# Second network's second product in an attention and two-network kernel: seven products for eight on the last two superblocks, in a phase of its own

## The chip, the cores and the metric

One NeuronCore of one Trainium2 chip runs the whole kernel in one launch. The metric is device time in microseconds (us) of that core. Lower is better. The kernel before was timed in three runs: 848.94, 844.0 and 844.74 us, a median of 844.74.

## The reference, cut to what matters

The reference computes a linear attention over 2304 tokens (4 batches of 576), and puts the result through two feed-forward networks, one after the other. The change is in the last line of the second network.

```python
def _moe2_ref(x, w_in, w_out):            # x: 2304 x 512
    h = x @ w_in                          # 512 x 2048
    sp = np.where(h > 20.0, h, np.log1p(np.exp(np.minimum(h, 20.0))))
    g = h * np.tanh(sp)                   # "mish"
    return (g @ w_out).astype(np.float32) # 2048 x 512
```

The weights arrive as 64-bit floats; the kernel decodes them on the chip.

## The kernel before

**Precision.** TensorE multiplies in a rounded 32-bit type (`float32r`). Every operand is therefore split in two tiles, a rounded value (hi) and what the rounding left (lo), by `split` (L408): a copy that rounds (ACT or DVE), then a subtraction (DVE, seldom POOL). A product is three matmuls: hi·hi, hi·lo, lo·hi (`SPLIT`, L258). Decoded weights lie in the tiles `W` (L267): 16 tiles, one for each 128 of the 2048 hidden columns, each with a half for the first weight (`io` 0; in the second network ring and scratch) and a half for the second weight (`io` 1), hi and lo.

**Stages.** Attention runs first and in pieces beside the first network. The first network's first three token blocks (512 tokens each) run plainly (L933, L976). From then on the work is 32 steps, `n` = 0 to 31 (the loop at L1404). A step is one superblock of 768 tokens by 256 hidden columns (`NPR` = 8 steps to a superblock). Steps 0 to 7 are the last 768 tokens of the first network; steps 8 to 31 are the second network, superblocks 0, 1 and 2. The steps that the change treats differently are 16 to 31.

**A step.** The first matrix product of a step is cut in blocks of two by two, and takes seven block products where the plain rule has eight (`product`, L1154). Each has 6 matmuls of 384 columns. `after` (L1203) takes the sums out of PSUM on DVE (L1213) and ACT (L796); `activated` (L1179) applies the activation on ACT (L1185) and splits the result into the tiles `second` and `g`. Between the products of step n stand the matmuls of the second product for step n-1: `gemm_out2` (L1236), six groups `c` of 128 tokens, each 6 matmuls of 512 columns, which add up in six PSUM banks over the eight steps of a superblock:

```python
        def mm():
            for j in range(2):
                for i, (a, b) in enumerate(SPLIT):
                    nc.tensor.matmul(
                        out=bank_of(out_banks[c]),
                        lhsT=g_tile(n, j)[:, a, c * P : (c + 1) * P],
                        rhs=w_mm(2 * pr + j, 1, b, 0, 512),
```

After the eighth step, `out_evac` (L1299) copies a bank to SBUF and stores it.

**What a step loads.** The seven sums of blocks of the first weight are made earlier, kept in DRAM (`combos`) and streamed back in each superblock: three loads of 512 KB and one of 256 KB for a step (`ring_load`, L1132), into a ring of tiles that holds two steps. A load waits for the products of the step that used the tile before. The step's other operands, sums of token blocks, are made once a superblock (`x_load` L1042, `x_sums` L1063, `x_split` L1076).

**What sets the order.** The program does not issue as it is written. Every operation is recorded with the keys it reads and writes and a cost (`Plan`, L20). A list scheduler then orders all of them over the engines, six times over with different urgencies, and the order with the earliest planned end is issued (`best`, L169). On TensorE a common key, `spine`, keeps the steps' matmuls in the order of the text; the other engines' order is the scheduler's. All DMAs go through SP's one queue, in order (`dma`, L328). A DMA, or an engine's instruction, that waits holds up what is queued behind it.

Of the kernel before, what the change touches and what calls it, by code (L numbers as in the profile page):

```python
# [210 lines left out]
def tile_attention_moe_moe(  # L211
# [55 lines left out]
    W = [const.tile([P, 2, 1024], F32R, name=f"W{i}") for i in range(NFC - NLATE)]  # L267
# [8 lines left out]
    combos = dram.tile([NFC, P, 3584], F32, name="combos")  # L276

# [38 lines left out]
    def f32(t):  # L316
        return t.bitcast(F32)

# [93 lines left out]
    def weight(m, io, fc):  # L412
# [3 lines left out]
        late = [("late",)] if fc >= NFC - NLATE else []  # L416
        split(
            512,
            lambda: W[fc][:, io, 0:512],
            lambda: W[fc][:, io, 512:1024],  # L420
# [14 lines left out]
    def keep(j, n):  # L435
# [4 lines left out]
        w0, w1 = [lambda k=k: f32(W[2 * j + k][:, 0, :]) for k in range(2)]  # L440
# [12 lines left out]
    def combine1(j, n):  # L453
# [5 lines left out]
        w0, w1 = [lambda k=k: f32(W[2 * j + k][:, 0, :]) for k in range(2)]  # L459
# [85 lines left out]
    def w_mm(fc, io, part, c, n=P):  # L545
        return W[fc][:, io, part * 512 + c * P : part * 512 + c * P + n]
# [450 lines left out]
    second = []  # L997

    def pool_first():
        sctx.close()  # L1000
        late = ctx.enter_context(tc.tile_pool(name="late", bufs=1, side="right", reuse_waits="tile"))
        W.extend(late.tile([P, 2, 1024], F32R, name=f"W{i}") for i in range(NFC - NLATE, NFC))
# [36 lines left out]
    def xf(i):  # L1039
        return f32(W[i][:, 0, 0 : 2 * NB])  # L1040

    def x_load(sb):  # L1042
        for i, (c, half) in enumerate(((0, 0), (1, 0), (0, 1), (1, 1))):
# [8 lines left out]
                w_keys(i),  # L1052
                lambda i=i: xf(i).rearrange("p (c n) -> p c n", c=2),
# [9 lines left out]
    def x_sums():  # L1063
        differ(2 * NB, ta, lambda: xf(1), lambda: xf(0), w_keys(0) + w_keys(1), tak)
        differ(2 * NB, tb, lambda: xf(3), ta, w_keys(3) + tak, tbk)

    def operand(k, a):
        if k in (2, 3):
            fc = ((4, 5), (6, 7))[k - 2][a]
            return W[fc][:, 0, 0 : 2 * NB].rearrange("p (c n) -> p c n", c=2)  # L1070
# [5 lines left out]
    def x_split(k, fresh):  # L1076
        old, new = [], [("second",)]
        if fresh and k in (2, 3):
# [9 lines left out]
        if k == 3:  # L1088
            for c in range(2):
# [3 lines left out]
                    NB, t, lambda cut=cut: xf(3)[:, cut], lambda cut=cut: xf(1)[:, cut], w_keys(1) + w_keys(3) + new, tk  # L1093
# [12 lines left out]
            0: (lambda: xf(0), w_keys(0)),  # L1106
            1: (tb, tbk),
            2: (lambda: xf(2), w_keys(2)),
            4: (ta, tak),
            5: (tb, tbk),  # L1110
            6: (lambda: xf(3), w_keys(3)),
# [10 lines left out]
        if k == 1:  # L1122
            differ(2 * NB, tb, tb, lambda: xf(2), w_keys(2), tbk)

    def ring(n, u):
        if u < 3:
            fc = 8 + 3 * (n % 2) + u
            return fc, 0, 512, w_keys(fc)
        fc = NFC - 2 + n % 4 // 2
        return fc, n % 2 * 512, 256, [("W", 0, fc, n % 2)]  # L1130

    def ring_load(n, u):  # L1132
        if n >= NP:
            return
        fc, at_, half, keys = ring(n, u)
        dma(
            P * half * 8,
            [("combo", n if n < NPR else NPR + n % NPR, u)],
            keys,
            lambda: f32(W[fc][:, 0, at_ : at_ + 2 * half]),  # L1140
            lambda: combos[n if n < NPR else NPR + n % NPR][:, u * 1024 : u * 1024 + 2 * half],
        )
# [11 lines left out]
    def product(n, k):  # L1154
        u, q = PLACE[k]
        fc, at_, half, wk = ring(n, u)
        key = bank(n, k)

        def mm():
            for cc in range(2):  # L1160
                for i, (a, b) in enumerate(SPLIT):
                    w = at_ + a * half + q * 256 + cc * P
                    nc.tensor.matmul(  # L1163
                        out=bank_of(key)[:, 0:NB],
                        lhsT=W[fc][:, 0, w : w + P],
# [13 lines left out]
    def activated(n, j, half, t, tk):  # L1179
# [8 lines left out]
        act(NB + 1540 * first, tk + ([] if first else tables), tk + (tables if first else []), fn)  # L1188
        gk = [[("gg", n % 2, j, half, a)] for a in range(2)]
# [13 lines left out]
    def after(n, k):  # L1203
# [5 lines left out]
        def added(name, of, op=ALU.add):  # L1209
# [255 lines left out]
```

## Time and profile before

| | |
|---|---|
| median of three runs (lowest, highest) | 844.74 us (844.0, 848.94) |
| the profiled execution's own time | 846.24 us |
| its span, first to last instruction | 844.5 us |
| TensorE busy, granted clock | 830.8 us, 0.997 |
| VectorE (DVE), ScalarE (ACT), GpSimd (POOL) busy | 570.6, 430.6, 14.8 us |
| moved by DMA | 153.89 MB |

The engines run side by side, and each works through its own queue in order. The span is set by the chain of work that ends last; an engine's busy time matters only where that chain runs through it. Matmuls overlap in the records, so what one matmul costs is read from the distance between the starts of two, not from its recorded length.

### The profile page before, as it was taken

To read this page: it belongs to the slowest core of one execution; us is meant where nothing else is said; L and a number is where in the kernel's file an instruction comes from. 1 tells how busy PE (TensorE), PEld (TensorE's weight loads), DVE (VectorE), ACT (ScalarE), POOL (GpSimd) and SP (SyncE) were. 2 spreads that over 40 slices of the span, in tenths; PEclk is the share of its full clock that TensorE was granted. 3 is DMA by queue.
4 is the path that set the end of the run, shared out by engine and by line. 5 is a ranking of instruction groups with operands and counts; after the bars stand their busy time and mean duration, and the time that the engine had idled before them with its cause. 6 is when DMAs were issued, how large, how long until landed. Compare 5 with 4: busy or idle time off the path is not lost.

```text
span 844.5 us, 12240 instructions
## 1 busy us (share of the span) xinstructions
PE 830.8 (98%) x4463; PEld 715.7 (85%) x4463; DVE 570.6 (68%) x1038; ACT 430.6 (51%) x851; POOL 14.8 (2%) x21
## 2 busy tenths in 40 slices
PE   8999999999999999999999999999999999999997
PEld 7787677887778888999999998898898998988985
DVE  6999995979969777566779889456333365334331
ACT  5988894345555445444556755344423345323222
POOL 0001010010000000000000000000000000000000
PEclk9999999999999999999999999999999999999998
DMA  9687762635476577865888887445534335434202
GB/s 272 172 249 258 215 220 95 202 110 161 128 212 222 192 260 250 252 223 174 288 282 273 282 267 224 131 140 183 177 113 118 120 113 156 156 112 137 76 1 75
DMA packets 99451, 153.89 MB, mean 182 GB/s; under 512 B 35136, under 2 KB 68672, under 8 KB 99392
## 3 DMA queue, kind: packets, MB, share of 16 engines
q1 hardware_dynamic: 99392, 153.12, 58.4%
q8 instruction: 35, 0.57, 0.3%
q14 instruction: 24, 0.20, 0.1%
HBM read 112.72 MB, written 40.37 MB: 181 GB/s over the span
## 4 chain that ended last, share of the span: by engine, by line
PE 81%; DVE 13%; DMA 2%; issue 2%; ACT 1%; SPq 0%; ACTq 0%; DVEq 0%
PE at L1163 27%; PE acc L1243 16%; PE acc L976 10%; PE h L933 9%; PE h L1243 8%; PE acc L1268 5%; PE h L1268 3%; DVE dec L400 2%; DVE dec L405 2%; DVE dec L393 1%; DVE W L339 1%; DVE gt L952 1%; DVE pmt L594 1%; PE at L852 1%; PE acc L612 1%
## 5 line engine op out<-in xcount | busy, mean ns | idle before, releaser
L1163 PE MATMUL at<-xt,W 128*128 128x384 f32 x954 | 191.3, 335 | 0.0
L1163 PEld LDWEIGHTS at<-xt,W 128*128 128x128 f32 x954 | 169.6, 188 | 12.6
L933 PE MATMUL h<-xt,W 128*128 128x512 f32 x576 | 149.4, 401 | 2.7 <-DVE W L339 1.0
L976 PE MATMUL acc<-g,W 128*128 128x512 f32 x576 | 146.4, 397 | 0.4 <-DVE W L339 0.4
L933 PEld LDWEIGHTS h<-xt,W 128*128 128x128 f32 x576 | 105.6, 188 | 28.6 <-DVE W L339 1.9
L1185 ACT ACTIVATE stage<-stage 128x384 f32<-128x384 f32 x94 | 49.2, 524 | 156.8 <-DVE stage L1213 156.7
L976 PEld LDWEIGHTS acc<-g,W 128*128 128x128 f32 x576 | 106.5, 188 | 23.6 <-DVE W L339 0.8
L1243 PE MATMUL acc<-W,second 128*128 128x512 f32 x432 | 115.6, 394 | 0.0
L1243 PEld LDWEIGHTS acc<-W,second 128*128 128x128 f32 x432 | 79.7, 188 | 10.6
L1213 DVE TENSOR_TENSOR stage<-at,stage 128x384 f32<-128x384 f32 x91 | 50.0, 554 | 50.9 <-PE at L1163 50.6
L1163 PE MATMUL at<-W,W 128*128 128x384 f32 x372 | 74.7, 335 | 0.0
L339 DVE TENSOR_TENSOR second<-stage,second 128x384 fp32r<-128x384 f32 x70 | 38.9, 556 | 44.3 <-ACT second L347 44.1
L1163 PEld LDWEIGHTS at<-W,W 128*128 128x128 f32 x372 | 65.9, 188 | 2.9
L1243 PE MATMUL h<-W,second 128*128 128x512 f32 x216 | 57.6, 394 | 0.0
L347 ACT ACTIVATE g<-gt 128x512 fp32r<-128x512 f32 (+1 forms) x56 | 34.4, 614 | 38.4 <-PE acc L976 33.3
L339 DVE TENSOR_TENSOR g<-gt,g 128x512 fp32r<-128x512 f32 (+1 forms) x52 | 34.6, 665 | 21.0 <-ACT g L347 20.5
L1185 ACT ACTIVATE gt<-gt 128x384 f32<-128x384 f32 x34 | 17.8, 524 | 58.1 <-DVE gt L1213 58.0
L356 ACT ACTIVATE dec<-raw 128x512 f32<-128x512 f32 x63 | 42.0, 667 | 7.3 <-DMA raw<-in_moe_w_in_dram 3.9
L947 ACT ACTIVATE gt<-h 128x512 f32<-128x512 f32 x48 | 28.5, 594 | 32.3 <-PE h L933 30.3
L405 DVE CUSTOM_DVE_ANT_0 dec<-raw,dec 128x1024 uint16<-128x1024 uint16 x64 | 43.7, 683 | 1.5
L1243 PEld LDWEIGHTS h<-W,second 128*128 128x128 f32 x216 | 39.9, 188 | 5.4
L400 DVE SCALAR_TENSOR_TENSOR dec<-raw,dec 128x512 int32<-128x512 int32 x64 | 43.8, 685 | 0.7
(141 smaller groups left out, 1098.5 us busy)
## 6 DMA issues: line engine op xcount, KB each, us to landing
W<-combos SPq DMA_DIRECT2D x96, 512.0 KB, 3.7
raw<-in_moe_w_in_dram SPq DMA_DIRECT2D x32, 512.0 KB, 5.0
raw<-in_moe_w_out_dram SPq DMA_DIRECT2D x32, 512.0 KB, 4.7
combos<-raw SPq DMA_DIRECT2D x32, 512.0 KB, 3.3
W<-combos SPq DMA_DIRECT2D x32, 256.0 KB, 3.7
combos<-raw SPq DMA_DIRECT2D x24, 256.0 KB, 3.5
kt<-in_k_dram SPq DMA_DIRECT2D x16, 288.0 KB, 4.3
W<-x2d SPq DMA_DIRECT2D x12, 384.0 KB, 3.9
```

The costliest lines, as they stand in the source:

```text
L339: return lambda: engine.tensor_tensor(out=out(), in0=in0(), in1=in1(), op=op)
L347: (ACT, act_ns(n), lambda: nc.scalar.activation(out=out(), in_=in_(), func=AF.Copy), False),
L356: (ACT, act_ns(512), lambda: nc.scalar.activation(out=out, in_=in_, func=AF.Copy, scale=scale), False),
L400: lambda: nc.vector.scalar_tensor_tensor(out=a, in0=hi_w, scalar=-0x80000000, in1=a, op0=ALU.bitwise_and, op1=ALU.bitwise_or),
L405: dve(512, [rl], [da], lambda: nc.vector.tensor_tensor(out=a, in0=a, in1=lo_w, op=ALU.add), pair=True)
L933: nc.tensor.matmul(out=h(), lhsT=w_mm(fc, 0, a, cc), rhs=x_of(t)[:, cc, b, :], start=cc == 0 and i == 0, stop=cc == NCC - 1 and i == 2,)
L976: nc.tensor.matmul(out=acc[dm][:, 0:nb], lhsT=w_mm(fc, 1, a, dm), rhs=g_of(n)[:, b, :], start=fc == 0 and i == 0, stop=fc == NFC - 1 and i ...
L1163: nc.tensor.matmul(out=bank_of(key)[:, 0:NB], lhsT=W[fc][:, 0, w : w + P], rhs=operand(k, b)[:, cc, :], start=cc == 0 and i == 0, stop=cc ...
L1185: nc.scalar.activation(out=t(), in_=t(), func=AF.Mish if n >= NPR else AF.Gelu_apprx_sigmoid)
L1213: dve(NB, [key, sk], tk, lambda: nc.vector.tensor_tensor(out=t(), in0=in0(), in1=in1(), op=op))
L1243: nc.tensor.matmul(out=bank_of(out_banks[c]), lhsT=g_tile(n, j)[:, a, c * P : (c + 1) * P], rhs=w_mm(2 * pr + j, 1, b, 0, 512), start=pr = ...
L1268: nc.tensor.matmul(out=o, lhsT=w_mm(2 * n + j, 1, a, dm), rhs=g_tile(n, j)[:, b, lo:hi], start=n == 0 and j == 0 and i == 0 and (c < 4 or ...
```

## The change

Superblocks 1 and 2 of the second network (steps 16 to 31) no longer run the second product between the first's products. The activations of a superblock are kept in float32 (`kept`, in the memory of the second weights, whose tiles are turned over one after the other to `quads`), and after the eight steps a phase of its own, `out_phase`, does the second product. It too is cut in blocks of two by two and takes seven products where the plain rule has eight: each runs over all 8 column pairs `pr`, 3 chunks of 128 tokens and 3 matmuls, with 256 columns moving where there were 512. The left operand of each is a sum or difference of kept blocks (`combined`), split anew (`left`) as soon as the product before has read the place. The right operands (four sums of weight blocks and two plain blocks) are made in steps 10 to 16 (`right_parts`), stored to DRAM (`outs`) and streamed through the same ring as the first weights, four loads of 512 KB a product; the seventh (`right_kept`) stays in SBUF. The seven results are summed on DVE into two rows of SBUF tiles, `u` and `v` (`out_done`), and stored in pieces of 256 columns. From step 18 on the first product's sums rotate over four PSUM banks instead of two. `W` becomes `w_first` and `w_second`.

```diff
+    def ring(g, u, out=False):
+        fc = 8 + 3 * (g % 2) + u if u < 3 else NFC - 2 + g % 2
...
+    for sb in range(2, NSB):
+        RINGS += [("in", sb * NPR + i) for i in range(NPR)] + [("out", name) for name in LOADED]
...
     def bank(n, k):
...
+        if n > NSEQ + 1:
+            return (("at", 0), ("at", 1), ("h", 0), ("h", 1))[(7 * n + k) % 4]
...
             activated(n, j, half, t, tk)
+            if n >= NSEQ and k == 6:
+                either(
+                    NB,
+                    ALU.subtract,
+                    lambda: kept(pr, 0, 1),
+                    lambda: kept(pr, 0, 0),
+                    lambda: kept(pr, 0, 1),
+                    [kept_key(pr, 0, 0)],
+                    [kept_key(pr, 0, 1)],
+                )
+                left("ps3", pr)
+                combined("ps2", pr)
...
+    def left(name, pr):
+        place = (pr, *PLACES[name])
+        split(
+            NB,
+            lambda: slot(pr, 0),
+            lambda: slot(pr, 1),
+            lambda: kept(*place),
...
+    def combined(name, pr):
...
+        either(
+            NB,
+            op,
+            lambda: kept(*to),
+            lambda: kept(pr, *one),
+            lambda: kept(pr, *two),
...
+    def right_parts(j, base):
...
+        for i, (w, q, k) in enumerate(((w0, 0, 0), (w1, 0, 1))):
+            dma(
+                P * 2048,
+                wk[k],
+                [("outs", i, j, a) for a in range(2)],
...
+        for k, w in enumerate((w0, w1)):
+            either(
+                512,
+                ALU.add,
...
+        for out, one, two, keys in (
+            (b11, b12, b11, rk[:1]),
+            (b12, b22, b12, rk),
+            (b22, b22, b11, rk),
+            (b21, b22, b21, rk[1:]),
+        ):
+            either(256, ALU.subtract, lambda out=out: out, lambda one=one: one, lambda two=two: two, keys, keys)
+        for k in range(2):
+            cut = slice(k * 512, k * 512 + 512)
+            split(
+                512,
...
+        for a, (src, keys) in enumerate(((f32(t), tk), (r, rk))):
+            for h in range(2):
+                dma(
+                    P * 2048,
...
+    def out_product(sb, m, pr, chunks):
...
+        def mm():
+            for c in chunks:
+                at_ = 256 * (c == 1 and not alone)
+                for i, (a, b) in enumerate(SPLIT):
+                    nc.tensor.matmul(
+                        out=bank_of(banks[c])[:, at_ : at_ + 256],
+                        lhsT=slot(pr, a)[:, c * P : c * P + P],
+                        rhs=rhs(b),
...
+    def out_phase(sb):
+        n = (sb + 1) * NPR + NPR - 1
+        for m in range(len(SEQUENCE)):
+            last = sb == NSB - 2 and m == 6
+            for chunks in ((0,), (1,), (2,)) if last else ((0, 1, 2),):
+                for pr in range(NPR):
+                    out_product(sb, m, pr, chunks)
+                    if m == 6:
+                        continue
+                    name = SEQUENCE[m + 1]
+                    left(name, pr)
+                    if name in ("p11", "p12"):
+                        combined("ps1" if name == "p11" else "ps4", pr)
+                    if pr % 2:
+                        ring_load(group_out(n, m) + 2, pr // 2)
+                for c in chunks if last else (0, 2):
+                    out_done(sb, m, c)
...
+    RIGHTS = {10: ((0, 2),), 11: ((1, 2),), 12: ((2, 2),), 13: ((3, 2),), 14: ((4, 0),), 15: ((5, 0),), 16: ((6, 0), (7, 0))}
...
-            if kk == 0 and n >= 2:
+            if kk == 0 and 2 <= n < NSEQ + 2:
                 gemm_o(n - 2, 5)
-            if kk >= 2 and n >= 1:
+            if kk >= 2 and 1 <= n < NSEQ + 1:
                 gemm_o(n - 1, kk - 2)
...
+        for j, base in RIGHTS.get(n, ()):
+            right_parts(j, base)
...
+        if n >= NSEQ and n % NPR == NPR - 1:
+            out_phase(n // NPR - 1)
```

`NSEQ` is 16. The order in which the instructions are issued is the scheduler's again, over the whole program. Three places of it follow; the names are tiles (`acc`, `h` and `at` are PSUM banks, `W` or `wi` the tiles of the ring, `quad` the kept activations, `stage` and `gt` temporaries).

TensorE, step 31 before: products of the first matrix (384 columns) alternate with groups of the second (512 columns).

```order
L1163 MATMUL at_108<-xt,W_446 128x384 x6
L1243 MATMUL h_102<-W_78,second_2813 128x512 x3
L1243 MATMUL h_102<-W_79,g 128x512 x3
L1163 MATMUL at_107<-xt,W_79 128x384 x6
L1243 MATMUL h_103<-W_78,second_2813 128x512 x3
L1243 MATMUL h_103<-W_79,g 128x512 x3
```

TensorE after the change, the end of step 23 and the start of the first phase:

```order
L1203 MATMUL at_112<-xt,wi_451 128x384 x6
L1203 MATMUL h_106<-xt,wi_80 128x384 x6
L1203 MATMUL h_107<-xt,wi_453 128x384 x6
L1456 MATMUL acc_101<-wi_76,second_2824 128x256 x6
L1456 MATMUL acc_102<-wi_76,second_2824 128x256 x3
L1456 MATMUL acc_101<-wi_76,second_2824 128x256 x6
L1456 MATMUL acc_102<-wi_76,second_2824 128x256 x3
```

The 384-column products now stand in a row, and so do the 256-column ones; the matmuls that stood between them are gone.

SP's DMA queue, ring loads for steps 21 and 22 after the change (a wait on PE is the wait for the ring tile, a wait on DMAHW one for an earlier DMA):

```order
L335 DMA wi_451<-combos 128x1024 [waits DMAHW1_49,PE_49]
L335 DMA wi_80<-combos 128x1024 [waits DMAHW2_49,PE_49]
L335 DMA wi_453<-combos 128x512 [waits DMAHW3_49,PE_49]
L335 DMA outs<-raw_88 128x2x256 [waits DMAHW4_49]
L335 DMA wi_76<-combos 128x1024 [waits DMAHW5_49,PE_49]
L335 DMA wi_78<-combos 128x1024 [waits DMAHW6_49,PE_49]
L335 DMA wi_77<-combos 128x1024 [waits DMAHW7_49,PE_49]
L335 DMA outs<-wo_454 128x2x256 [waits DMAHW0_49]
L335 DMA outs<-wo_454 128x2x256 [waits DMAHW1_49]
L335 DMA outs<-wo_454 128x2x256 [waits DMAHW2_49]
```

Before, only loads stand there; now stores of `right_parts` stand among them, as late as step 20.

DVE, step 20 after the change:

```order
L1255 TENSOR_TENSOR quad_5059<-gt,at_112 128x384 [waits PE_49]
L344 TENSOR_TENSOR raw_88<-wo_454 128x512 [waits DMAHW4_49]
L1255 TENSOR_TENSOR quad_5059<-h_106,gt 128x384 [waits DVE_49,PE_49]
L344 TENSOR_TENSOR raw_88<-raw_88 128x256 [waits DVE_49] x2
L344 TENSOR_TENSOR quad_5059<-quad_5059 128x384 [waits Activation_49]
```

Before, DVE has here only the additions out of PSUM and the subtractions of the splits. Now an instruction of `right_parts` stands between two of the additions that free PSUM banks, and it waits for a store (DMAHW4) to have read its buffer.

## Rows read from the trace of the kernel before

**Rows 1.** The page: span; busy us of engines; GB/s in 40 equal slices.

```profile
PE 830.8 (98%) x4463; PEld 715.7 (85%) x4463; DVE 570.6 (68%) x1038; ACT 430.6 (51%) x851; POOL 14.8 (2%) x21
...
GB/s 272 172 249 258 215 220 95 202 110 161 128 212 222 192 260 250 252 223 174 288 282 273 282 267 224 131 140 183 177 113 118 120 113 156 156 112 137 76 1 75
```

**Rows 2.** The page: the chain that ended last, shares of the span by engine.

```profile
PE 81%; DVE 13%; DMA 2%; issue 2%; ACT 1%; SPq 0%; ACTq 0%; DVEq 0%
```

**Rows 3.** The chain in order of time: start us, us, what (L1163 pairs: one a step).

```profile
407.01 1.43 PE h L1268 x12
...
580.80 2.08 PE at L1163 x12
...
815.40 2.08 PE at L1163 x12
...
835.42 2.73 PE h L1243 x12
```

**Rows 4.** Timeline of TensorE: start us, us, engine line op out<-in xcount.

```profile
473.24 1.55 PE L1243 MATMUL acc<-W,second 128*128 128x512 f32 x6
474.63 1.21 PE L1163 MATMUL at<-W,W 128*128 128x384 f32 x6
...
829.82 0.84 PE L1243 MATMUL acc<-W,second 128*128 128x512 f32 x3
830.50 0.84 PE L1243 MATMUL acc<-W,g 128*128 128x512 f32 x3
```

**Rows 5.** Groups of instructions, second product's matmuls: busy us, mean ns; idle before.

```profile
L1243 PE MATMUL acc<-W,second 128*128 128x512 f32 x432 | 115.6, 394 | 0.0
...
L1243 PE MATMUL h<-W,second 128*128 128x512 f32 x216 | 57.6, 394 | 0.0
...
L1243 PE MATMUL acc<-W,g 128*128 128x512 f32 x144 | 40.9, 392 | 0.0
...
L1243 PE MATMUL h<-W,g 128*128 128x512 f32 x72 | 20.4, 392 | 0.0
```

**Rows 6.** Windows: stretch, us, PE, PEld, DVE, ACT, POOL busy, PEclk, DMA share, GB/s.

```profile
345.56:471.32 125.76, 125.76 (x720) 117.05 (x719) 94.11 (x182) 66.78 (x126) 0.99 (x1) 1.00 0.76 251
471.32:486.96 15.64, 15.64 (x79) 14.06 (x79) 12.02 (x23) 9.60 (x18) 0.00 (x0) 1.00 0.88 284
...
643.36:659.00 15.64, 15.64 (x79) 14.06 (x79) 5.92 (x11) 4.69 (x9) 0.00 (x0) 1.00 0.39 117
...
46.00:133.00 87.00, 83.88 (x442) 63.65 (x441) 85.11 (x158) 73.01 (x181) 6.75 (x4) 1.00 0.71 220
```

**Rows 7.** The page: DMA issues, KB each, median us from issue to landing.

```profile
W<-combos SPq DMA_DIRECT2D x96, 512.0 KB, 3.7
...
combos<-raw SPq DMA_DIRECT2D x24, 256.0 KB, 3.5
```

**Rows 8.** Groups of DVE and ACT instructions: busy us, mean ns; idle before.

```profile
L1213 DVE TENSOR_TENSOR stage<-at,stage 128x384 f32<-128x384 f32 x91 | 50.0, 554 | 50.9 <-PE at L1163 50.6
...
L339 DVE TENSOR_TENSOR second<-stage,second 128x384 fp32r<-128x384 f32 x70 | 38.9, 556 | 44.3 <-ACT second L347 44.1
L347 ACT ACTIVATE second<-stage 128x384 fp32r<-128x384 f32 x69 | 36.1, 523 | 1.8
...
L339 DVE TENSOR_TENSOR raw<-dec,raw 128x512 fp32r<-128x512 f32 x40 | 26.7, 682 | 0.8 <-ACT raw L347 0.6
...
L339 DVE TENSOR_TENSOR dec<-dec,dec 128x256 f32<-128x256 f32 x14 | 6.0, 425 | 0.1
```

**Rows 9.** Timeline of the last microseconds: start us, us, engine line op.

```profile
832.00 9.79 SPq L330 DMA_DIRECT2D out_dram<-dec  x16
...
838.22 0.38 ACT L1315 ACTIVATE dec<-h 128x256 f32<-128x256 f32 x1 [0.98 <-PE h L1243]
838.64 0.42 DVE L1314 COPY dec<-h 128x256 f32<-128x256 f32 x1 [0.94 <-ACT dec L1315]
```

More of the change, by code (lines that the diff above doesn't have):

```diff
@@ L545, in w_mm @@
     def w_mm(fc, io, part, c, n=P):
[L546 removed]
+        return wt(fc, io)[:, part * 512 + c * P : part * 512 + c * P + n]
     def k_tile(u):
@@ L1155, in product @@
         u, q = PLACE[k]
-        fc, at_, half, wk = ring(n, u)
+        fc, half, wk = ring(group_in(n), u)
         key = bank(n, k)
@@ new lines, in right_kept, with fn, b22 @@
+    def right_kept(j):
+        def fn():
+            nc.scalar.activation(
+                out=b22(j).rearrange("p (a f) -> p a f", a=2),
+                in_=halves(f32(wt(2 * j + 1, 1)))[:, :, 1, :],
+                func=AF.Copy,
+            )
+        plan.op(
+            [(ACT, act_ns(512), fn, False)],
+            [("W", 1, 2 * j + 1, a) for a in range(2)],
+            [("W", 0, j // 2, j % 2)],
+        )
+    def b22(j):
+        return wt(j // 2, 0)[:, j % 2 * 512 : j % 2 * 512 + 512]
@@ new lines, in turned_over, with fn @@
+    def turned_over(i):
+        def fn():
+            pool = pools[0] if i == NFC // 4 - 1 else const
+            quads.append(pool.tile([P, 4096], F32, name=f"quad{i}", tag=f"wo{i}"))
+        keys = [("kept", pr, j, half) for pr in (2 * i, 2 * i + 1) for j in range(2) for half in range(2)]
+        old = [("W", 1, 4 * i + c, a) for c in range(4) for a in range(2)]
+        plan.op([(NONE, 0.0, fn, False)], [], old + keys + [("xf", i), ("quads",)])
+    SEQUENCE = ("ps3", "p11", "p12", "ps2", "ps1", "p22", "ps4")
@@ new lines, in rows_out @@
+    def rows_out(sb, half, dmh, c, src, keys):
+        lo_ = sb * SB + half * NB + c * P
+        end = lo_ + P
+        first = lo_
+        while lo_ < end:
+            t = max(t for t in range(NBLK) if BASE[t] <= lo_)
+            col, p0 = divmod(lo_ - BASE[t], SIZES[t] // NCT)
+            n = min(SIZES[t] // NCT - p0, end - lo_)
+            dst = out[BASE[t] : BASE[t + 1], :].rearrange("(p c) e -> p c e", c=NCT)[p0 : p0 + n, col]
+            dma(
+                n * 1024,
+                keys,
+                [],
+                lambda dst=dst: dst[:, dmh * 256 : dmh * 256 + 256],
+                lambda r=lo_ - first, n=n: src[r : r + n],
+            )
+            lo_ += n
@@ L1404, in tile_attention_moe_moe @@
     for n in range(NP):
+        if n == NSEQ:
+            for j in range(NPR - 2):
+                right_kept(j)
+            for i in range(NFC // 4 - 1):
+                turned_over(i)
         for kk in range(7):
```

258 lines of the change are left out of this document (207 added, 51 removed).

## The prediction

> **What bounds the kernel now.** I read the page first. TensorE is busy for 830.8 of 844.5 us, DVE for 570.6, and DMA moves under 160 GB/s in nearly all of the last third, where superblocks 1 and 2 lie [rows 1]. The chain that ended last says the same: 81% of the span is TensorE [rows 2]. The stretch that the change touches is TensorE from one end to the other: its second-product groups show no idle time before them [rows 5], and the windows show it busy in 15.64 of 15.64 us, with DVE at 5.92 of 15.64 and DMA at 117 GB/s [rows 6]. So what counts is the work in TensorE's queue, as long as the others keep up.
>
> Three distances between starts price that work. Twelve 384-column matmuls take 2.08 us, so a product of six takes 1.04 [rows 3]. Three 512-column matmuls take 830.50 - 829.82 = 0.68 us, 226.7 ns each [rows 4]. Twelve 256-column matmuls, which the first network already has at L1268, take 1.43 us, 119.2 ns each [rows 3]. A step is (815.40 - 580.80) / 15 = 15.64 us [rows 3]; its parts, seven products and six groups of six 512-column matmuls, give 7.28 + 8.16 = 15.44. The missing 0.20 us lies at the alternation of shapes: a group between products takes 474.63 - 473.24 = 1.39 us, where six alone take 1.36 [rows 4].
>
> **The change, part by part.** I count from 580.80, the second and third product of step 16, to the end of TensorE's work, 835.42 + 2.73 = 838.15 [rows 3]: 257.35 us before.
>
> *TensorE.* Of the 864 matmuls of 512 columns [rows 5], 576 go: two superblocks of 288, 130.6 us. In come 2 phases x 7 products x 8 pairs x 9 matmuls = 1008 of 256 columns, 120.2 us. Columns fall by one eighth, but each matmul carries the same overhead and there are more of them, so only 10.4 us are left of it. The alternation goes too: from step 17 or 18 on products follow products, and the phase holds one shape. The new sum from the same point: 6 products of step 16 (6.24), its five groups of step 15 (6.95), step 17 with the last group (8.67), steps 18 to 31 (14 x 7.28 = 101.92), the phases (120.16): 243.9 us. That is **13.4 us less**: 10.4 from the matmuls and 3.0 from the alternation. This price leaves little doubt: 384 and 512 columns put 256 at 120.0 ns by a straight line, against 119.2 measured.
>
> Of the pitch, the Trainium skill ("TensorE: Matmul & The Clock Gate", Back-to-back issue gap) says that a warm matmul takes its columns at 2.4 GHz plus 2.5 ns. By that the term would be 576 x 215.8 - 1008 x 109.2 = 14.2 us instead of 10.4. The trace shows 13 ns above the columns for every shape, so the sum goes by the rows.
>
> *The end.* Now the last two half-bank copies end at 838.64 + 0.42 = 839.06, and SP issues stores until 841.79, 16 in 9.79 us or 0.61 each [rows 9]: four or five after the last copy. The changed kernel ends with one addition of 256 columns and two stores. That saves between 0 and 1.5 us; I take **1.0**, two issues less with something off for a DVE queue that may be late.
>
> *DVE and ACT.* A step of 16 to 31 has seven additions out of PSUM (0.554) and three subtractions (0.556): 5.5 us of DVE in the step's 7.28, and six ACT operations of about 0.52, 3.1 us [rows 8]. A phase has 48 subtractions of `left`, 16 of `combined` (64 x 0.556 = 35.6) and eight sums of 512 and 256 columns (8 x (0.682 + 0.425) = 8.9): 44.5 us of DVE in 7 x 8.58 = 60.1; ACT has 48 copies, 25 us. The first phase also holds the next superblock's operands, by the same rows some nine subtractions of twice 384 columns and four of 384, 12 us: 57 of 60. Each `left` has the other seven pairs of the product, 7.5 us, to get ready. TensorE's matmuls cover all of this, so it costs nothing, but only while DVE's queue moves.
>
> *`right_parts`.* Eight times 4 x 0.682 + 4 x 0.425 = 4.4 us of DVE [rows 8], 35 us in all, and 48 stores of 256 KB, spread by the scheduler over steps 10 to 24. Steps 10 to 15 are 15.64 us long and have room. Steps 16 to 20 are shorter, and there DVE's order has instructions of `right_parts` ahead of PSUM additions, and they wait until a store has read their buffer; a store of this size lands 3.5 us after its issue [rows 7].
>
> *DMA.* A step now streams 1.835 MB in 7.28 us, 252 GB/s; a phase product 2.1 MB in 8.58, 244 GB/s. By SP's order the densest part is from the third product of step 16 to the end of the phase's fourth product, 98 us: six step groups (11.0 MB), six phase groups (12.6), 17 stores of `right_parts` (4.5) and five output stores (1.3), 29.4 MB, 300 GB/s. Steps 24 to 31 ask 15.2 MB in 58.2 us, 261 GB/s. The trace holds 284 GB/s over a whole step with TensorE full, at a DMA share of 0.88, that is about 320 at a share of 1; over a longer stretch, 126 us, it shows 251 at a share of 0.76 [rows 6]. A ring tile's load is issued a step and more ahead, 10.4 us or more in the steps, against 3.7 us to landing [rows 7]: some 7 us may be lost before TensorE stands.
>
> What these waits cost TensorE the trace of before cannot show. The lower end is nothing: in the stretch from 345.56, with 251 GB/s, DVE at 94 of 126 us and `combos` stores in the same queues, TensorE never stood [rows 6]. The upper end, for stores alone, is 10.8 us, worked out in the first rival below; a DMA rate that gives way is a rival of its own. I take **3.5 us**, a third of the way, since that stretch is the nearest row.
>
> *The first 330 us.* The scheduler reshuffles them as well, without other work. Between 46 and 133 us TensorE is busy 83.88 of 87 with DVE at 85.11 [rows 6], so it loses 3.1 us to waits there; another order could win or lose as much. I take **0**.
>
> *The sum.* -13.4 - 1.0 + 3.5 + 0 = -10.9. The profiled execution took 846.24 us, 1.74 more than its span of 844.5. The span becomes 833.6 and that execution 835.3; the median of the runs lies 1.5 lower, at **833.8 us**.
>
> **The rivals.**
>
> *DVE's queue stands behind stores.* Six DVE instructions in steps 15 to 20 wait for a store of `right_parts` before additions that free PSUM banks; four are in steps up to 17, where the sums still rotate over two banks. Each can hold DVE for 3.5 us [rows 7], of which the other bank hides one product, 1.04 us, and in steps 18 and 20 the other three banks 3.1. That is 4 x 2.5 + 2 x 0.4 = 10.8 us: -13.4 - 1.0 + 10.8 = -3.6, so **841.1 us**. For it speaks that the order puts these rows between additions; against it, that the stores were issued some time before, so that part of the 3.5 us has passed. The Trainium skill ("DMA: Bandwidth & Descriptors", Latency and other measured facts) gives 0.2 us for an access to device memory on average and 2 us at high load. By that each of these waits would grow by 1.8 us, and the rival would come to 4 x 4.3 + 2 x 2.2 = 21.6 us, 852 us; the stretch at 284 GB/s, with TensorE full, does not bear that out.
>
> *DMA sets the pace.* The rings, not TensorE, end the steps and the phase. At a sustained rate of r, the 29.4 and 15.2 MB take 44.6 MB / r in place of 98 + 58.2 us, and 7 us of lead may be used up. At 284 GB/s that is 157 us, and nothing is lost. The gain of 14.4 is gone at 44.6 / (98 + 58.2 + 7 + 14.4) = 251 GB/s; below that the kernel is slower. At 240 GB/s it is 185.8 us, 22.6 lost, a net of +8.2: **852.9 us**. For it speaks that no stretch of over 100 us shows more than 251 [rows 6]; against it, that the share there was 0.76, so the queue had nothing to do for a quarter of the time.
>
> That the change does not do what it says I leave out: TensorE's new order shows the 256-column matmuls in a row and none of 512 between the products.
>
> **How the numbers follow.** I give the forecast 0.63, DVE behind stores 0.28, DMA 0.09. A difference of under 1%, 8.4 us, is about what a measurement of this kernel cannot tell from none. The forecast's own range is 829.5 (no wait at all, and a little won early) to 837; a part of it, 0.05, stays within 1%. The first rival is within 1% but for 0.03, where only a few waits bite. So faster is 0.63 - 0.05 + 0.03 = 0.61, the same 0.05 + 0.25 = 0.30, slower 0.09. The range reaches over the first rival's 841.1 with early waits added: 829.5 to 844.
>
> **What would show it.** In the changed profile: steps 18 to 23 and 24 to 31 at 7.28 us each, a phase product at 8.58, both phases at 60, and no idle time before the 256-column matmuls. TensorE standing in steps 16 to 20, released by DVE additions whose engine waited for a DMA, means the first rival. Ring loads that land later than 10 us after their issue, and matmuls released by DMA, mean the second. If a run of 256-column matmuls paces above 125 ns, the main term is wrong. A start of step 8 that moved by more than 3 us makes the early term wrong.

## The result, and the profile after

The changed kernel takes 833.44 us (median of four runs, 831.88 to 835.7) against 844.74 (844.0 to 848.94, four runs beside it). The ratio is 0.9859, with a 95% interval of 0.9825 to 0.9892: faster, by 1.4%. The profiled execution took 833.88 us with a span of 832.1, 12.4 less than the span of before.

The page of the changed kernel, busy time and GB/s in 40 slices, and the chain's shares; it answers [rows 1, 2]:

```profile
PE 817.9 (98%) x4897; PEld 727.2 (87%) x4897; DVE 668.9 (80%) x1247; ACT 459.8 (55%) x916; POOL 17.9 (2%) x22
...
GB/s 265 193 247 256 212 233 51 207 115 130 135 198 262 201 241 256 211 220 221 249 240 307 270 256 252 276 233 254 232 289 277 277 367 281 181 263 274 289 240 58
...
PE 82%; DVE 8%; ACT 4%; DMA 4%; issue 1%; SPq 1%; DVEq 0%; ACTq 0%
```

TensorE is still the chain, at 82%. DVE's share rose from 68 to 80% and the last third now moves 181 to 367 GB/s but for its last slice, yet neither came to the front.

TensorE's timeline of before, step 0 and step 16's second product (start us, us, engine, line, operation, tiles, count):

```profile
331.28 1.23 PE L1163 MATMUL at<-xt,W 128*128 128x384 f32 x6
...
580.64 1.21 PE L1163 MATMUL at<-xt,W 128*128 128x384 f32 x6
```

The same view after the change (L1203 is the first matrix's product, L1456 the phase's), with a row of the early part and the last matmuls; it answers [rows 3, 4]:

```profile
90.22 0.43 PE L857 MATMUL at<-qT,kv 128*128 128x64 f32 x2 [1.09 <-ACT qT L837]
...
333.91 1.23 PE L1203 MATMUL at<-xt,wi 128*128 128x384 f32 x6
...
583.27 1.21 PE L1203 MATMUL at<-xt,wi 128*128 128x384 f32 x6
...
649.23 6.63 PE L1456 MATMUL acc<-wi,second 128*128 128x256 f32 x54
...
709.70 2.25 PE L1203 MATMUL at<-xt,wi 128*128 128x384 f32 x12
...
767.95 6.63 PE L1456 MATMUL acc<-wi,second 128*128 128x256 f32 x54
774.41 2.32 PE L1456 MATMUL acc<-wi,g 128*128 128x256 f32 x18
...
827.69 0.88 PE L1456 MATMUL h<-wi,g 128*128 128x256 f32 x6
```

Three differences of these rows make the whole result. Step 0 starts 2.63 us later, and step 16 is later by the same 2.63, so nothing moved between. From step 16's second product to TensorE's end, 827.69 + 0.88 = 828.57, it is 245.30 us; before it was 838.15 - 580.64 = 257.51 [rows 3]: 12.2 less. From there to the end of the span it is 3.5 us where it was 6.35. 2.6 - 12.2 - 2.8 = -12.4, the difference of the spans.

The windows of steps 16 to 23, first phase, steps 24 to 31 and second phase, with two early stretches ahead (columns as in [rows 6]):

```profile
90.00:93.00 3.00, 2.78 (x9) 2.23 (x10) 3.00 (x5) 2.67 (x6) 0.00 (x0) 0.69 0.68 188
93.00:96.00 3.00, 3.00 (x14) 2.43 (x13) 2.91 (x7) 1.70 (x3) 0.00 (x0) 0.74 0.51 173
...
583.27:649.23 65.96, 65.87 (x367) 63.96 (x366) 49.02 (x97) 28.21 (x56) 0.00 (x0) 1.00 0.82 261
649.23:709.70 60.47, 60.47 (x506) 60.47 (x505) 48.53 (x90) 32.62 (x63) 4.78 (x3) 1.00 0.84 303
709.70:767.95 58.25, 58.25 (x339) 58.25 (x338) 43.06 (x82) 23.79 (x47) 0.00 (x0) 1.00 0.80 250
767.95:828.57 60.62, 60.62 (x505) 60.42 (x504) 42.43 (x84) 27.60 (x55) 0.00 (x0) 1.00 0.63 205
```

TensorE is busy in all of the last three stretches, with DMA at 303 GB/s in one of them and DVE at 48.5 of 60.5 us.

The groups and the DMA issues say the same: no idle time before the new matmuls [rows 5], and loads that land in 4.5 and 5.7 us where it was 3.7 [rows 7], still in time.

```profile
L1203 PE MATMUL at<-xt,wi 128*128 128x384 f32 x732 | 144.4, 335 | 0.1
...
L1456 PE MATMUL acc<-wi,second 128*128 128x256 f32 x738 | 91.0, 283 | 0.0
...
wi<-combos SPq DMA_DIRECT2D x96, 512.0 KB, 4.5
wi<-outs SPq DMA_DIRECT2D x48, 512.0 KB, 5.7
```

SP's queue around the first phase's start, and SP and DVE at the end, which answers [rows 9]:

```profile
638.36 0.42 SPq L335 DMA_DIRECT2D out_dram<-dec  x1
644.95 0.88 SPq L335 DMA_DIRECT2D outs<-raw  x2
645.93 3.59 SPq L335 DMA_DIRECT2D wi<-outs  x5
...
660.09 0.37 SPq L335 DMA_DIRECT2D outs<-raw  x1
660.56 1.86 SPq L335 DMA_DIRECT2D wi<-outs  x4
...
820.51 9.34 SPq L335 DMA_DIRECT2D out_dram<-raw  x12
...
828.61 0.42 DVE L1497 TENSOR_TENSOR raw<-raw,h 128x256 f32<-128x256 f32 x1 [2.45 <-PE h L1456]
```

At the end one addition stands after the last matmul, done at 829.03, and SP issues its last store by 829.85, 0.8 us later; before, it was 2.7 us after the last copy. The first five rows matter for the rivals. SP stood for 6.1 us, from 638.78, before two stores of weight sums, and the phase's second ring tile (the first of the five loads at 645.93) was issued only behind them. TensorE used it at 649.23 + 18 x 0.12 = 651.4, 5.5 us after the issue, when such loads took 5.7 in the median. This one landed 4.7 us after its issue, at 650.6, 0.8 us before its use. The store at 660.09 had held SP for 9.0 us, waiting for ACT; the load behind it landed at 665.3, 1.2 us before the phase's third product needed it, at 649.23 + 2 x 8.64 = 666.5.

### The profile page after: what moved, and what is told of

It is laid out like the page before. It is cut to its first block, busy times and chain, and to the rows that moved or that the text cites. A ratio compares the mean times of both kernels' runs of the same rounds, so it can differ in the third digit from the quotient of the medians.

```text
span 832.1 us, 13739 instructions
## 1 busy us (share of the span) xinstructions
PE 817.9 (98%) x4897; PEld 727.2 (87%) x4897; DVE 668.9 (80%) x1247; ACT 459.8 (55%) x916; POOL 17.9 (2%) x22
## 4 chain that ended last, share of the span: by engine, by line
PE 82%; DVE 8%; ACT 4%; DMA 4%; issue 1%; SPq 1%; DVEq 0%; ACTq 0%
PE at L1203 21%; PE acc L1456 14%; PE acc L981 11%; PE h L938 10%; PE h L1203 7%; PE acc L1586 5%; PE acc L1561 5%; PE h L1586 3%; PE h L1561 3%; DMA raw<-in_moe_w_in_dram 1%; DMA raw<-in_moe_w_out_dram 1%; DVE pmt L599 1%; PE at L857 1%; DVE dec L410 1%; ACT qt L777 1%
## 5 line engine op out<-in xcount | busy, mean ns | idle before, releaser
L938 PE MATMUL h<-xt,wi 128*128 128x512 f32 x576 | 147.6, 399 | 1.4 <-DVE gt L957 0.9
L981 PE MATMUL acc<-g,wo 128*128 128x512 f32 x576 | 147.2, 400 | 0.4 <-ACT stage L801 0.4
L1203 PE MATMUL at<-xt,wi 128*128 128x384 f32 x732 | 144.4, 335 | 0.1
L1203 PEld LDWEIGHTS at<-xt,wi 128*128 128x128 f32 x732 | 128.8, 188 | 6.4 <-DVE quad L1255 0.4
L938 PEld LDWEIGHTS h<-xt,wi 128*128 128x128 f32 x576 | 106.0, 188 | 26.0 <-DVE gt L957 1.3
L981 PEld LDWEIGHTS acc<-g,wo 128*128 128x128 f32 x576 | 107.0, 189 | 24.0 <-ACT stage L801 0.8
L1456 PE MATMUL acc<-wi,second 128*128 128x256 f32 x738 | 91.0, 283 | 0.0
L1456 PEld LDWEIGHTS acc<-wi,second 128*128 128x128 f32 x738 | 89.7, 192 | 0.0
L1203 PE MATMUL at<-wi,wi 128*128 128x384 f32 x294 | 58.3, 335 | 0.0
L1203 PEld LDWEIGHTS at<-wi,wi 128*128 128x128 f32 x294 | 51.9, 188 | 1.6 <-ACT stage L801 0.2
```

The lines of the kernel that those rows point to most:

```text
L938: nc.tensor.matmul(out=h(), lhsT=w_mm(fc, 0, a, cc), rhs=x_of(t)[:, cc, b, :], start=cc == 0 and i == 0, stop=cc == NCC - 1 and i == 2,)
L981: nc.tensor.matmul(out=acc[dm][:, 0:nb], lhsT=w_mm(fc, 1, a, dm), rhs=g_of(n)[:, b, :], start=fc == 0 and i == 0, stop=fc == NFC - 1 and i ...
L1203: nc.tensor.matmul(out=bank_of(key)[:, 0:NB], lhsT=wt(fc, 0)[:, w : w + P], rhs=operand(k, b)[:, cc, :], start=cc == 0 and i == 0, stop=cc ...
L1456: nc.tensor.matmul(out=bank_of(banks[c])[:, at_ : at_ + 256], lhsT=slot(pr, a)[:, c * P : c * P + P], rhs=rhs(b), start=pr == 0 and i == 0 ...
```

## The experiments

**Eight products in the phase.** The phase, the kept activations and the streaming stay; the second product is done with the plain eight block products, four rounds of 512 moving columns, without sums of weights or of activations.

```diff
-    SEQUENCE = ("ps3", "p11", "p12", "ps2", "ps1", "p22", "ps4")
...
+        for m in range(4):
...
-                        rhs=rhs(b),
+                        rhs=wt(fc, 0)[:, b * 512 : b * 512 + 512],
```

> The phase of its own is kept, but with the plain eight block products: 512 columns moving, 288 matmuls a phase, the second weights streamed as they are, no sums of weight blocks and none of kept blocks. If the gain is TensorE's work (columns and matmuls), a phase takes 288 x 0.2267 = 65.3 us instead of 60.5, steps 18 to 23 stay at 7.28, and the kernel is 9.6 us slower than the changed one, about 843, give or take 3 for the order of the first 330 us. If the phase itself (no alternation of shapes) brings most of the gain, the phase stays under 62 and the kernel under 837. If streaming limits, the phase takes over 70.

Measured: 843.0 us (841.33 to 844.94, ten runs; ratio to before 0.9969, interval 0.9956 to 0.9983). TensorE's timeline of this run:

```profile
580.18 1.21 PE L1196 MATMUL at<-xt,wi 128*128 128x384 f32 x6
...
601.66 1.31 PE L1196 MATMUL at<-xt,wi 128*128 128x384 f32 x6 [0.46 <-DVE quad L1248]
...
824.58 0.94 PE L1324 MATMUL acc<-wi,g 128*128 128x512 f32 x3 [0.58 <-DMA wi<-outs]
...
834.90 1.52 PE L1324 MATMUL h<-wi,g 128*128 128x512 f32 x6
```

And the window of its first phase:

```profile
646.49:711.81 65.32, 65.32 (x290) 54.05 (x289) 19.67 (x33) 16.92 (x32) 0.32 (x1) 1.00 0.83 271
```

The stretch from 580.18 to 836.42 is 256.2 us, against 257.5 before and 245.3 with seven products. This run has two waits of TensorE that the changed kernel has not, 0.46 us at 601.66 and 0.58 at 824.58, so the difference of the two stretches says too much for the seven products. The first phase has no wait in either run: 65.32 us with eight products, 60.47 with seven. So the seven products bring 4.85 us a phase, 9.7 of the 12.2, and the phase by itself the other 2.5: four fifths of the change is arithmetic on TensorE.

**Only the last superblock changed.** Superblock 1 keeps the old form, superblock 2 has the phase.

```diff
-    NSEQ = 2 * NPR
+    NSEQ = 3 * NPR
...
-    for sb in range(2, NSB):
+    for sb in range(3, NSB):
```

> Only the last superblock (steps 24 to 31) goes the new way. If each superblock gains by itself, the stretch from the second product of step 16 to the end of TensorE's work loses half of the 12.2 us of the full change, 6.1, the microseconds after TensorE's end stay at 3.5, and the kernel comes to about 837 to 839. If the gain lies at the end of the kernel alone, it stays at 834 or below; if the first of the two phases brings it, it goes to 843 or more.

Measured: 836.61 us (835.55 to 837.69; ratio 0.9892, interval 0.9869 to 0.9915). Two rows of TensorE's timeline:

```profile
579.03 1.21 PE L1203 MATMUL at<-xt,wi 128*128 128x384 f32 x6
...
829.84 0.88 PE L1456 MATMUL h<-wi,g 128*128 128x256 f32 x6
```

From step 16's second product at 579.03 to TensorE's end at 830.72 it is 251.7 us: 5.8 of the 12.2, one superblock's half, and the end is as short as with both (834.3 - 830.7 = 3.6). The total looks better than half because step 0 started at 329.69, 4.2 us ahead of the changed kernel.

**Two PSUM banks instead of four.** From step 18 on the sums rotate over two banks, as they do before.

```diff
-        if n > NSEQ + 1:
-            return (("at", 0), ("at", 1), ("h", 0), ("h", 1))[(7 * n + k) % 4]
```

> The four PSUM banks of steps 18 to 31 are taken back to two; nothing else changes. If four banks are what keeps DVE's queue off TensorE's path, a product that needs two additions (0.55 + 0.47 us and the waits around them) no longer fits behind the next one's 1.04 us, and each of the 14 steps grows from 7.28 to 8 to 10 us: 10 to 35 us more, 843 to 868. If two banks are enough, as the single step 17 suggests, the steps stay at 7.28 and the kernel within 2 us of 833.4.

Measured: 843.71 us in one run. The longest of TensorE's waits between 600 and 655 us (who waited for whom: us in total, times, longest):

```profile
PEld at L1201 <- DVE quad L1253: 5.3, 14, 0.5
```

From step 16's second product at 581.83 to the first phase at 652.35 it is 70.5 us instead of 65.96, and from there to TensorE's end at 838.15 another 6.5 more. Steps grow by some 0.8 us each, since product after product now asks for its bank before DVE has emptied it. The second bank pair is a necessary part, worth 11 us in this one run. The kernel before had two banks and no such wait; there the groups of 512 columns stood between the products, which left DVE that time.

**Ten passes of the scheduler.** Another order of the same work.

```diff
-    PASSES = 6
+    PASSES = 10
```

> The scheduler gets ten urgencies to choose from instead of six; the operations are the same. If the 2.6 us by which step 0 starts later than in the kernel before are a draw of the scheduler's order, step 0 starts at another time, 331 to 333, and the total follows it by the same amount, 830 to 833, with the same distance from step 0 to the end of TensorE's work (494.7). If the new layout of the weights in SBUF delays the start, step 0 stays at 333.9 within 0.3.

Measured: 833.74 us (832.18 to 834.44). Step 0 at 333.41 instead of 333.91, and 498.2 us from there to the end as in the changed kernel. It moved too little to tell whether the 2.6 us lost early belong to the change.

**Every ring load twice.** A test of the second rival, DMA's rate.

```diff
-    def ring_load(g, u):
+    def ring_load(g, u, again=False):
...
         fc, half, keys = ring(g, u, kind == "out")
+        if g >= NSEQ + 2 and not again:
+            ring_load(g, u, True)
```

> Every load of the ring from group 18 on (three for a step, four for a product of the phase) is issued twice, the same bytes to the same tile; nothing else changes, and TensorE's work is the same. A step then streams 3.67 MB in place of 1.835, a phase product 4.19 in place of 2.1. Theory (DMA's rate would set the pace if asked for twice as much, and what it then holds is its sustained rate): at 300 to 330 GB/s a step of 18 to 31 takes 11.1 to 12.2 us instead of 7.28 and a phase product 12.7 to 14.0 instead of 8.64, together some 110 to 140 us more, TensorE waits on DMA, and the quotient of bytes and time says how far the 252 GB/s that the change asks for stayed from the limit. Rival (there is room for twice as much): under 5 us more.

Measured: 939.65 us in one run, a span of 937.5, 105.4 more than the changed kernel, a little under the expected 110 to 140. Its window over the stretch, the longest entry of TensorE's waits, and the two longest of SP's queue in that window:

```profile
618.00:900.00 282.00, 213.05 (x1308) 198.17 (x1306) 155.22 (x286) 91.64 (x177) 0.00 (x0) 0.94 0.96 336
```
```profile
PE acc L1458 <- DMA wi<-outs: 25.1, 25, 1.9
```
```profile
SPq L335 <- DMA wi<-outs: 93.4, 38, 4.7
SPq L335 <- DMA wi<-combos: 67.0, 32, 5.5
```

Asked for twice as much, DMA holds 336 GB/s over 282 us at a share of 0.96. This is not shown to be its limit: the second load of a pair goes to the same tile and waits until the first has landed, and for that SP's queue stood 160 of the 282 us, a wait that the test itself brought in. As a lower bound it is enough. It lies a third above the 250 that the changed kernel's steps take, and above the 303 of its first phase; the prediction's rival, with its turning point at 251, is out.

**The kernel before, with two passes.** The same edit as with ten passes, made to the kernel before, and two in place of six.

> The kernel before the change, with the scheduler's passes cut from six to two, so that the order issued is another draw; no work changes. Theory (the 2.6 us that the changed kernel loses in the first 330 us are a draw of the scheduler's order and no effect of the change): step 0 starts 1 to 3 us off the 331.28 of before, on either side, the spacing of 15.64 us from there on is the same, and the total moves by what step 0 moved. Rival (the early loss belongs to the change, its layout of memory or its loads): step 0 stays within 0.3 us of 331.28.

Measured: 847.05 us (845.62 to 849.5, ten runs; ratio 1.0024, interval 1.0011 to 1.0038). TensorE's timeline, step 0:

```profile
333.78 1.23 PE L1163 MATMUL at<-xt,W 128*128 128x384 f32 x6
```

Step 0 is 2.50 us later than in the kernel before, without any change of the work, and the span is longer by 2.6. So the order alone moves step 0 by as much as the changed kernel lost.

**The last product not cut.** The three chunks of the very last product alternate as in the others.

```diff
...
-            last = sb == NSB - 2 and m == 6
+            last = False
```

> The very last product of the kernel is not cut in three chunks of its own: the matmuls of the three chunks alternate as in the other products, and the additions and all six stores come after the last of them. The work is the same. Theory (the end is priced by the additions and the stores' issues that are left after the last matmul): from the last matmul to the end of the span 5.5 to 6.5 us in place of 3.5, two additions and six issues at 0.4 to 0.6 us each; the total grows by 2 to 3, less what the early order draws. Rival (the landing of the last store alone sets the end): within 0.5 us of 3.5.

Measured: 835.77 us (835.48 to 836.46; ratio 0.9896, interval 0.988 to 0.9912), 2.3 more than the changed kernel. Its last matmuls and stores:

```profile
825.41 2.32 PE L1454 MATMUL acc<-wi,g 128*128 128x256 f32 x18
827.41 1.02 DVE L1495 TENSOR_TENSOR raw<-raw,acc 128x512 f32<-128x512 f32 x2 [6.97 <-PE acc L1454]
...
828.12 3.19 SPq L335 DMA_DIRECT2D out_dram<-raw  x6
```

The last matmul ends at 825.41 + 2.32 = 827.7, so 6.0 us are left to the end of the span, 833.7, in place of 3.5: inside the expected 5.5 to 6.5, and much the same as the 6.35 before the change. The end is priced by the stores that still have to be issued after the last matmul.

**Stores of weight sums twice.** A test of the first rival: `right_parts` issues its four stores of sums a second time, to the same place.

```diff
-        for a, (src, keys) in enumerate(((f32(t), tk), (r, rk))):
+        for a, (src, keys) in 2 * list(enumerate(((f32(t), tk), (r, rk)))):
```

> Every store of the weight sums that are made in steps 10 to 16 is issued twice, four of 256 KB more for each of the eight pairs, so that their buffers are held longer and 8.4 MB more stand in the same queue; nothing else changes. Theory (DVE's instructions behind those stores have a wide margin): from step 16's second product to the first phase stays within 1 us of 65.96, and steps 10 to 16 keep 15.64. Rival (the prediction's first rival was near, with DVE held up to 3.5 us at six places): TensorE stands in steps 15 to 20, released by DVE whose engine waited for a DMA, and the stretch grows by 3 to 11 us.

Measured: 862.73 us in one run. From step 16's second product (587.49) to the first phase (673.08) it is 85.6 us, 19.6 more: the rival, beyond its 11 us, and the theory of a wide margin falls. But between 440 and 700 us TensorE waited longer for ring loads (8.6 us) than for DVE (5.3), and SP's queue stood 15 times, 20.0 us, for an earlier store of the same place. That wait is one the test itself had brought in, so a second form was needed.

**The second copy to a place of its own.** As above, but the second store goes to a tensor that nobody reads, so that no store waits for a store.

```diff
+    spare = dram.tile([6, P, NFC // 2, 2, 256], F32, name="spare")
...
+                    [("spare", 2 + 2 * h + e, j, a) for e in range(2)],
```

> The four stores of each pair's weight sums are made twice again, but the second copy goes to a DRAM tensor of its own that nobody reads, so that it waits for no earlier store. DVE's buffers are held as long as in the run that stored twice to one place and as many bytes move; what is gone is the wait of a store for a store in SP's queue. Theory (in that run TensorE waited for ring loads behind such stores in SP's queue, and DVE has a wide margin): from step 16's second product to the first phase 66 to 68 us, and the kernel within 3 us of the changed one. Rival (the held buffers or the bytes cost the time): some 15 to 29 us more, as there.

Measured: 854.15 us in one run, with a step 0 at 331.32. From 580.78 to the phase at 666.38 it is again 85.6 us. So the theory fell once more: it was not the wait of a store for a store. SP's and TensorE's timelines of this run:

```profile
623.62 0.70 SPq L336 DMA_DIRECT2D wi<-combos  x1
632.74 0.36 SPq L336 DMA_DIRECT2D spare<-raw  x1
...
635.97 0.94 SPq L336 DMA_DIRECT2D wi<-combos  x2
```
```profile
634.40 1.20 PE L1204 MATMUL at<-xt,wi 128*128 128x384 f32 x6
639.93 2.26 PE L1204 MATMUL at<-xt,wi 128*128 128x384 f32 x6 [4.32 <-DMA wi<-combos]
641.98 2.12 PE L1204 MATMUL h<-xt,wi 128*128 128x384 f32 x6
```

And the waits of SP's queue between 604 and 660 us, and a window just after the wait:

```profile
SPq L336 <- DVE raw L345: 15.0, 3, 8.3
```
```profile
640.00:643.00 3.00, 3.00 (x10) 3.00 (x11) 1.22 (x3) 0.18 (x2) 0.00 (x0) 0.50 1.06 378
```

SP had a store at the head of its queue from 624.3 to 632.7, waiting for DVE to make the sum; the next ring loads stood behind it and went out only from 635.97. TensorE, through with what it had, stood 4.32 us for one. In those 8.3 us DVE waited for no store; it came to the sum at 632.02, after ACT had rounded at 630.83. Its waits for earlier stores to have read their buffers came later (0.81 us at 636.26, 2.56 at 650.84). The waits of TensorE in the stretch add up to 11.1 us; of the rest of the 19.6 some 7 went at a lower clock, an estimate from the granted clock of its windows. In the window shown it is 0.50, and six 384-column matmuls take 2.05 us instead of 1.04. DMA's rate did not bring the long wait about: it was 244 GB/s at a share of 0.72 from 600 to 636 us. How much is due to buffers held longer and how much to the order that the scheduler drew for the added stores, these two runs don't separate.

**Three more orders of the changed kernel**: the scheduler's first, sixth and seventh pass.

```diff
-    PASSES = 6
+    PASSES = 1
```
```diff
-        return min(found)[2]
+        return found[5][2]
```

The third has seven passes and `found[6]`.

> The changed kernel with the order of the scheduler's first pass. No work changes. Theory (what the first 330 us give or take is the order drawn, and the rest does not depend on it): step 0 starts between 329 and 335, from step 0 to the end of the span 498 us as in the changed kernel, and the total moves by what step 0 moved. Rival (the change's new instructions also hang on the order): the stretch from step 0 on grows by more than 1.5 us, since stores or loads stand otherwise in the queues.

> The changed kernel with the order of the scheduler's sixth pass, the one that the kernel before used of its own. No work changes. Theory: step 0 starts between 329 and 335, from step 0 to the end 498 us, and the total follows step 0. Rival: with another order of stores and loads the stretch from step 0 on grows by more than 1.5 us.

> The changed kernel with a seventh pass of the scheduler, whose order is issued. No work changes; it is tried as a version that may beat both kernels. Theory (order alone moves step 0 and puts waits of one or two microseconds here and there): step 0 between 329 and 335, no wait of TensorE over 2 us after it, the total between 830 and 836. Rival (an order can also put a store of weight sums ahead of loads in SP's queue, so that TensorE stands as with the doubled stores): 3 us or more of waits for ring loads, and a total above 837.

Measured: 844.07 us (842.65 to 847.29), 834.25 (833.41 to 835.87) and 833.98 (833.34 to 837.3). The first pass loses 10.6 us, the whole gain, to its order. Its TensorE timeline, and a window behind the wait:

```profile
262.17 2.93 PE L981 MATMUL acc<-g,wo 128*128 128x512 f32 x6 [2.18 <-ACT stage L801]
...
341.16 1.23 PE L1203 MATMUL at<-xt,wi 128*128 128x384 f32 x6
```
```profile
264.00:268.00 4.00, 4.00 (x11) 3.10 (x10) 4.00 (x8) 1.96 (x4) 0.00 (x0) 0.52 0.59 235
```

Step 0 starts at 341.16, outside the expected 329 to 335, and from there on it takes 842.4 - 341.16 = 501.2 us, 3.0 more than the changed kernel; 1.4 of these are waits in step 0 for an operand, 0.6 a wait for a load in the phase, and about 1 was not followed. So its rival holds. The sixth pass starts step 0 at 331.16, 2.75 early, and gives nearly all of it back: 832.0 - 331.16 = 500.8, with TensorE's waits

```profile
PE acc L1586 <- DVE second L344: 1.6, 1, 1.6
PE at L1203 <- DVE gt L1255: 0.4, 1, 0.4
```

at step 8. So the rival, a later stretch that hangs on the order, holds there too, though not by loads. The seventh pass starts step 0 at 334.29, has no wait from there on, and takes 498.2 us again. None of the three is faster than the changed kernel beyond what the runs tell apart.

## Why the prediction was right

The forecast of 833.8 us (829.5 to 844) met 833.44, and its mechanism holds. Its terms are partly wrong in size and made up for one another, so that a hit to 0.4 us is luck. In spans the forecast was 833.6 and the measurement 832.1; the medians lie closer because the profiled execution of before was 1.5 us above its median and that of the changed kernel 0.4. Term by term:

- *TensorE, -13.4.* It became -12.2. Steps 24 to 31 take 58.25 us, as worked out (8 x 7.28). The phases take 60.47 and 60.62 where 60.1 each was forecast: 54 matmuls in 774.41 - 767.95 = 6.46 us are 119.6 ns each, 72 in 60.47 / 7 = 8.64 us 120.0, so the straight line through 384 and 512 columns was the better price than the 119.2 of twelve in a short row. Over 1008 matmuls the 0.8 ns are 0.8 us. Steps 16 to 23 take 0.4 more than the sum. The eight-product run tells how the term splits: the matmuls gave 9.7 where 10.4 was forecast, and the alternation 2.5 instead of 3.0, so both parts were sized a little too large. The Trainium skill ("TensorE: Matmul & The Clock Gate", Back-to-back issue gap) gives columns at 2.4 GHz plus 2.5 ns for an isolated matmul, by which 256 columns would take an estimated 109.2 ns; for a stream in which each matmul has its own weight load it gives some 131 ns at 512 columns. The trace, where each matmul has its weight load, agrees with neither: 120.0 ns at 256 columns in rows of 504, and 226.7 at 512 [rows 4].
- *The end, -1.0.* It became -2.8, outside its bounds of 0 and -1.5. The step that was sized wrong is "two issues less": before, five stores were issued after the last copy, now two after the last addition, and that is 0.8 us in place of 2.7, 1.9 less. The other 0.9 was not in the term. The last addition ends 0.46 us after TensorE, where the last copy ended 0.91 after it, and the span ends 2.25 us after the last issue, where it was 2.71. Without the cut of the last product the end is 6.0 us, much as before.
- *Waits, +3.5.* It became 0, the lower bound. In the changed kernel TensorE waits for nothing from step 0 on. A third of the way to the upper bound was a guess between two mechanisms of which neither showed, and the nearest row, the stretch at 251 GB/s without a wait [rows 6], had said 0.
- *The first 330 us, 0.* It became +2.6, inside the bound of 3.1. The kernel before, drawn anew, loses 2.5 there too, and the changed kernel in its sixth order starts step 0 at 331.16, so the order alone can make the difference. Where the 2.6 us went is shown only in part: in the changed kernel TensorE stood 1.09 us at 90.22, then ran at a granted clock of 0.69 and 0.74 for 6 us, but it also stood longer than before later on (busy 30.31 us from 100 to 133 us and 68.04 from 190 to 260, where it was 31.37 and 69.30).

DVE's work in the first phase, forecast at 57 us, took 48.5: in a row its instructions start 0.48 us apart (616.71 and 617.19 in the changed kernel), less than the 0.556 recorded for one. It cost nothing either way.

*The first rival* did not happen, but it was nearer than its 0.28 let a reader think, and by another way. Between 440 and 700 us of the changed kernel DVE stood only once for a store of weight sums, 0.2 us. What was at risk is SP's queue: a store that waits for DVE's or ACT's part of the sum holds up ring loads behind it. There the changed kernel had waits of 6.1 and 9.0 us, and loads that landed 0.8 and 1.2 us before their use; with twice the stores, and the order drawn for them, the stretch took 19.6 us more. The prediction had both halves, the stores among the loads in SP's order and the 7 us of lead, and did not put them together; the lead that it took from loads issued 10.4 us ahead was for the steps, and the second ring tile of the first phase was issued 5.5 us ahead. *The second rival* was far off: 336 GB/s are to be had. Of its two signs one showed, ring loads that land later than 10 us after their issue (the slowest of the first phase took 10.7), but no matmul was released by DMA.

The four-bank rotation, which the prediction took for granted, is a condition of all this: without it nearly the whole gain is gone.

## What to carry to other kernels

Where one engine's queue is full from end to end, price a change by the distances between starts on that engine in long rows, and a term of a full per cent can be forecast to a tenth of itself; what surrounds it (the draw of a scheduler's order, the end, waits) needs its own bounds, and two of ours fell outside or on them. When a shape that gave another engine time is taken out, give that time back in another way, here with two more PSUM banks. In a single DMA queue look behind every store that waits for an engine: the loads that stand there are what the critical engine will miss.

## What the runs showed of the hardware that was not expected

A wait of TensorE can cost more than itself. After it had stood 1.09 us (changed kernel, 90.22), 2.18 us with two shorter ones before it (first pass, 262.17) and 4.32 us (stores aside, 639.93), the granted clock of the next stretches was 0.69 and 0.74, 0.52, and 0.50, that is at or toward 1.2 GHz in place of 2.4, for some 6, 6 and 10 us. In the last of these runs a stretch with 11.1 us of waits took 19.6 us more. Not every wait does it: in the kernel before with two passes TensorE stood for the same 1.09 us, at 92.50, and the granted clock behind it stayed at 1.00. What decides between the two the runs don't show. That run's window behind the wait (columns as in [rows 6]):

```profile
92.00:94.00 2.00, 1.50 (x8) 1.28 (x9) 2.00 (x4) 2.00 (x5) 0.00 (x0) 1.00 0.81 236
```

DMA held 303 GB/s over 60 us beside a full TensorE, and 336 over 282 us when every ring load was issued twice; the median time to landing of 512 KB was 3.7 us for the ring loads of the kernel before, and 4.5 and 5.7 for those of the changed one.
